# Shifted key and value copies moved from GpSimd to VectorE in a fused attention and mixer kernel

## The chip, the cores and the metric

The kernel runs on one core of a Trainium2 chip. The metric is the device time of one execution in microseconds (us). A core has five engines, each working through its own list of instructions strictly in order: TensorE (PE in the profile; its weight loads are listed apart as PEld), VectorE (DVE), ScalarE (ACT), GpSimd (POOL) and SyncE (SP). Engines wait for each other by semaphores. DMAs are issued from an engine's list too: here all loads from GpSimd's, the output stores from SyncE's.

## What is computed

First a windowed attention: 4 batches, 8 heads, 768 positions, head size 64. A query sees the first 8 positions (global) and the last 96 (local). Then a low-rank mixing over the positions and a two-layer channel network, both with a residual.

```python
scores = scale * np.matmul(q, k.transpose(0, 1, 3, 2))
is_global = pos[None, :] < int(n_global)              # 8
is_local = (rel >= 0) & (rel < int(n_local))          # 96
scores = np.where(keep, scores + bias, -1000000000.0)
a = softmax(scores)
x = a @ v                                             # heads side by side: (4, 768, 512)
h = xt @ U @ V                                        # xt: x with positions last; rank 32
u = x + h.transpose(0, 2, 1)
out = u + np.maximum(u @ w_ch1, 0.0) @ w_ch2          # 512 -> 2048 -> 512
```

(`softmax` stands here for the four lines that the reference writes out.)

## The kernel before

**Tiling.** The work of attention is cut into 16 pairs of heads, `pairs[i]`, four for each batch. The 768 positions are 6 blocks of 128. Since a query sees at most 96 positions back, a query block needs its own key block (the diagonal) and the last 96 positions of the block before it (the off-diagonal). The off-diagonal key block also has room for the global positions: `kP` (line 183) is a copy of the key tile `kT` in which, for each of 5 blocks, columns 32 to 127 are the block's own (line 184) and columns 0 to 31 are those of block 0 (line 185). `vp16` (lines 232 and 233) is the same for the values, in two buffers that alternate between pairs. Its source `v16` holds the values of 8 pairs, with a column of ones (line 141) that gives the softmax's sum.

**Steps of one pair**, by their functions: `load_pair` issues 6 DMAs from GpSimd (queries and keys, line 94, into `qkst`; values, line 100), each of which turns float32 into float16. `transposes` makes `qT` and `kT` on TensorE, which VectorE copies out of PSUM (lines 178 and 182), and then `kP`. `scores` multiplies (line 206) in three groups of blocks, the first of which reads `kP` alone; ScalarE takes the exponentials into `ep` (line 212), six activations for a pair. `mask` multiplies `ep` by the table of biases `expb` on VectorE (lines 224 and 227) and then makes `vp16`. `av` (lines 243 to 252) multiplies by the values, `norm` divides by the sum on VectorE (lines 266 and 270) and rounds to float16 on ScalarE (`x16`, line 275). `mix_tmp`, `mix_h` and `mix_t` are the low-rank step (lines 282 to 317).

**The channel network** is a queue of small pieces, `mlp_q`: for each batch 16 pieces of the first layer (`hps`, lines 329 and 335) and 24 of the second (`cps`, line 348, with the output at 354). `fill()` takes one piece off the queue and puts it between two steps of attention. The queue gets batch 0 at the end of iteration i = 4 of the main loop; before that, `fill()` does nothing. An iteration has ten calls of it, so a batch's 40 pieces go into four iterations. What is left at the end runs alone.

**The loop** (lines 372 to 400): iteration i does `mix_tmp` and `mix_h` of pair i - 1, `transposes` of pair i + 1, `av` and `norm` of pair i, `scores` and `mask` of pair i + 1, and `mix_t` of pair i - 1. Iteration -1 has only `transposes(0)`, `scores(0)` and `mask(0)`.

**Order.** For TensorE the order is that in which the code is written (line 369). On the other engines a scheduler lays the instructions out, from its own estimate of when each can start; within an engine nothing overtakes at run time. On GpSimd the program starts with the loads of pairs 0 to 3, the mixing matrices, the first layer's weights `w1_16` (line 152), pair 4 and the second layer's weights `w2_16` (line 155). The loads of a later pair wait until `transposes` has emptied a slot of `qkst`, which has 8.

**Tables.** `rel3` (lines 122 to 137) is built by GpSimd and VectorE, and `expb` from it on ScalarE (line 140); `mask` needs it.

In the profile names are shortened: `rel_106` is `rel3`, `v_81` is `v16`, `vp_82` is `vp16`, `w_16_79` and `w_16_80` are `w1_16` and `w2_16`, `x_...` with a number is `x16`, `tmp_...` with a number is `tmp16`, and `u_151` is `u16`.

Of the kernel before, what the change touches and what calls it, by code (L numbers as in the profile page):

```python
# [17 lines left out]
def kernel(  # L18
# [13 lines left out]
    nc = tc.nc  # L32
# [3 lines left out]
    P = 128  # L36
    G = 32
    DM = H * D
    NSB = S // P
    NPB = NSB - 1  # L40
# [7 lines left out]
    D1 = D + 1  # L48
# [20 lines left out]
    def ps_tp(name, dtype, cols):  # L69
        return psum.tile([P, cols], dtype, name=name, tag="tp", bufs=1)  # L70
# [95 lines left out]
    def transposes(i, which):  # L166
        stg = stage[i][which]
        tp = ps_tp("tp", FP16, NSB * P)
        for sb in range(NSB):
            nc.tensor.matmul(  # L170
                tp[:, sb * P:(sb + 1) * P],
                stg[:, sb].rearrange("s h d -> s (h d)"),
                ident16, is_transpose=True,
                start=(sb == 0), stop=(sb == NSB - 1),
            )
        if which == 0:
            qT = qkp.tile([P, S], FP16, name="qT", tag="qT")
            nc.vector.tensor_copy(qT, tp)
            qkT[i] = [qT]
        else:  # L180
            kT = qkp.tile([P, NSB, P], FP16, name="kT", tag="kT")
            nc.vector.tensor_copy(kT.rearrange("p n c -> p (n c)"), tp)  # L182
            kP = qkp.tile([P, NPB, P], FP16, name="kP", tag="kP")
            nc.gpsimd.tensor_copy(kP[:, :, G:P], kT[:, 0:NPB, G:P])  # L184
            nc.gpsimd.tensor_copy(  # L185
                kP[:, :, 0:G], kT[:, 0:1, 0:G].broadcast_to((P, NPB, G))
            )
            qkT[i] += [kT, kP]
# [28 lines left out]
    def mask(i):  # L217
        b, hp = pairs[i]
        ep = probs[i]
        for hi in range(2):  # L220
            h = 2 * hp + hi
            for j0, m in ((0, 2), (NPB, 1)):
                blk = ep[:, hi, j0:j0 + NPB]
                nc.vector.tensor_tensor(  # L224
                    blk, blk, expb[:, h, m:m + 1].broadcast_to((P, NPB, P)), ALU.mult
                )
        nc.vector.tensor_tensor(
            ep[:, :, NBK - 1], ep[:, :, NBK - 1], expb[:, 2 * hp:2 * hp + 2, 0], ALU.mult
        )
        vh = v16[:, i % VR]  # L230
        vp = vp16[:, i % 2]
        nc.gpsimd.tensor_copy(vp, vh[:, :, 0:NPB])
        nc.gpsimd.tensor_copy(vp[0:G], vh[0:G, :, 0:1].broadcast_to((G, 2, NPB, D1)))

    def av(i, hi):
        b, hp = pairs[i]
# [135 lines left out]
    for i in range(-1, NP + 1):  # L372
        if i + 6 < NP and i >= 0:
            load_pair(i + 6)
        if i >= 1:
            mix_tmp(i - 1)
            fill()
            mix_h(i - 1)
            fill()
        if i + 1 < NP:  # L380
            transposes(i + 1, 0)
            fill()
            transposes(i + 1, 1)
            fill()
        if 0 <= i < NP:
            av(i, 0)
            fill()
            av(i, 1)
            norm(i)
            fill()  # L390
        if i + 1 < NP:
            for ci in range(3):
                scores(i + 1, ci)
                fill()
            mask(i + 1)
        if i >= 1:
            mix_t(i - 1)
            fill()
            if i % NPAIR == 0:
                queue_batch(i // NPAIR - 1)  # L400
# [37 lines left out]
```

## Time and profile before

| what | us |
|---|---|
| median of two runs | 368.91 (368.76 to 369.07) |
| the profiled execution | 370.26 |
| its span, first to last instruction | 368.4 |
| TensorE busy | 269.3 (73%) |
| VectorE busy | 115.5 (31%) |
| ScalarE busy | 132.1 (36%) |
| GpSimd busy | 125.5 (34%) |

The granted TensorE clock is 1.00 throughout. The share of busy time hides that the run has stages. Here is the part of the page that cuts the span into 40 slices of 9.2 us; a digit is the busy share in tenths.

```profile
PE   1000055555559898999988999999899988777996
POOL 8994795674372507075060412011100000000000
```

TensorE does almost nothing in slices 2 to 5, is half busy in the next seven, and nine tenths busy from the thirteenth on; the digits 777 near the end are the last batch's first layer, which runs alone. GpSimd is busiest where TensorE is idle.

Rows of the other views read as follows. A timeline row: start, duration, engine, line, operation, output and input, shapes, count, and in brackets the idle time of the engine just before with what ended it. A row of the waits: who waited for whom, us in total, how many times, the longest.

### The profile page before, as it was taken

How to read it: one execution, taken by the hardware profiler on the slowest of the kernel's cores; microseconds unless marked ns; L12 is line 12 of the kernel's file. 1: busy time of each engine (PE TensorE's matmuls, PEld its weight loads, DVE VectorE, ACT ScalarE, POOL GpSimd, SP SyncE). 2: the span in 40 equal slices, each digit the busy share in tenths (PEclk: the TensorE clock that was granted, in tenths of full speed). 3: DMA queues.
4: the chain of work that ended last, by engine and by line, in shares of the span. 5: the costliest groups of instructions: out<-in, count | busy, mean ns of one | idle time of the engine just before them, and what ended most of it. 6: DMA issues, size and time to landing. Idle time of an engine off the chain costs nothing.

```text
span 368.4 us, 5118 instructions
## 1 busy us (share of the span) xinstructions
PE 269.3 (73%) x2080; PEld 147.0 (40%) x2080; DVE 115.5 (31%) x255; ACT 132.1 (36%) x265; POOL 125.5 (34%) x185
## 2 busy tenths in 40 slices
PE   1000055555559898999988999999899988777996
PEld 1000033444435455445444545545454544333442
DVE  1100054446442142555523254652322631000021
ACT  0400035432543654531547453235746200343100
POOL 8994795674372507075060412011100000000000
PEclk9999999999999999999999999999999999999999
DMA  9999999976591808297260601110000012000012
GB/s 69 105 122 204 187 171 60 64 52 41 38 67 11 55 0 55 39 120 71 62 44 0 41 5 59 59 47 11 0 2 0 34 53 85 2 0 0 30 57 85
DMA packets 82326, 20.34 MB, mean 55 GB/s; under 512 B 76640, under 2 KB 78720, under 8 KB 82304
## 3 DMA queue, kind: packets, MB, share of 16 engines
q0 software_dynamic: 78848, 13.74, 47.4%
q1 hardware_dynamic: 3456, 6.29, 4.6%
q8 instruction: 16, 0.26, 0.3%
q14 instruction: 6, 0.05, 0.1%
HBM read 27.46 MB, written 6.29 MB: 92 GB/s over the span
## 4 chain that ended last, share of the span: by engine, by line
PE 50%; ACT 17%; POOL 15%; DVE 8%; issue 5%; DMA 3%; POOLq 0%; ACTq 0%; DVEq 0%
PE cps L348 20%; PE hps L329 19%; ACT htr L335 13%; POOL qkst L94 7%; DMA w_16_79<-in_moe_w_ch_dram 3%; PE sc L206 3%; DVE ep L224 3%; POOL v_81 L100 3%; PE h_ps L294 2%; ACT ep L212 2%; PE tmp_ps L282 2%; DVE x_sb L299 2%; PE tp L170 1%; ACT uu L303 1%; POOL w_16_80 L155 1%
## 5 line engine op out<-in xcount | busy, mean ns | idle before, releaser
L329 PE MATMUL hps<-uT,w_16_79 128*128 128x384 f16 x512 | 105.4, 329 | 17.1 <-ACT htr L335 10.4
L348 PE MATMUL cps<-w_16_80,htr 128*128 128x512 f16 x384 | 93.1, 380 | 0.7 <-ACT htr L335 0.4
L335 ACT ACTIVATE htr<-hps 128x384 f16<-128x384 f32 x128 | 56.3, 487 | 82.6 <-PE hps L329 82.6
L329 PEld LDWEIGHTS <-w_16_79 128*128 128x128 f16 x512 | 49.4, 98 | 63.1 <-issue 38.7
L212 ACT ACTIVATE ep<-sc 128x512 f16<-128x512 f32 (+1 forms) x96 | 48.1, 563 | 50.0 <-PE sc L206 49.4
L224 DVE TENSOR_TENSOR ep<-ep,expb 128x640 f16<-128x640 f16 x64 | 30.6, 506 | 86.1 <-ACT ep L212 86.1
L94 POOL DMA_DIRECT2D qkst<-in_q_dram x32 | 26.9, 856 | 81.6 <-PE tp L170 80.8
L206 PE MATMUL sc<-qT,kP 64*128 64x128 f16 x160 | 12.7, 250 | 52.4 <-POOL kP L185 47.4
L348 PEld LDWEIGHTS <-htr 128*128 128x128 f16 x384 | 33.7, 98 | 35.3 <-issue 0.6
L354 DVE TENSOR_TENSOR osb<-cps,x_sb 128x512 f32<-128x512 f32 x24 | 16.6, 690 | 60.2 <-PE cps L348 59.7
L303 ACT ACTIVATE uu<-x_sb 128x768 f16<-128x768 f32 x16 | 13.5, 843 | 46.4 <-DVE x_sb L299 46.4
L206 PEld LDWEIGHTS <-kP 64*128 64x128 f16 x160 | 5.9, 108 | 56.1 <-POOL kP L185 49.4
L170 PE MATMUL tp<-ident_91,qkst 128*128 128x128 f16 x192 | 19.6, 251 | 11.7 <-POOL ident_91 L113 7.2
L100 POOL DMA_DIRECT2D v_81<-in_v_dram x32 | 26.8, 849 | 3.2 <-DMA w_16_79<-in_moe_w_ch_dram 3.0
L94 POOL DMA_DIRECT2D qkst<-in_k_dram x32 | 26.8, 861 | 2.8 <-PE tp L170 2.7
L184 POOL COPY kP<-kT 128x480 f16<-128x480 f16 x16 | 9.7, 608 | 50.8 <-DVE kT L182 50.8
L170 PEld LDWEIGHTS <-qkst 128*128 128x128 f16 x192 | 15.6, 113 | 17.4 <-issue 14.1
L299 DVE TENSOR_TENSOR x_sb<-x_sb,h_ps 128x768 f32<-128x768 f32 x16 | 15.3, 955 | 21.9 <-PE h_ps L294 21.9
L206 PE MATMUL sc<-qT,kT 64*128 64x128 f16 x192 | 15.0, 247 | 2.7 <-ACT ep L212 2.6
L270 DVE TENSOR_TENSOR x_sb<-ob,rcp 128x384 f32<-128x384 f32 x32 | 16.4, 552 | 0.0
L248 PE MATMUL ob<-vp_82,ep 128*128 128x65 f16 x160 | 16.1, 209 | 0.0
L252 PE MATMUL ob<-v_81,ep 128*128 128x65 f16 x160 | 16.1, 209 | 0.0
(103 smaller groups left out, 195.6 us busy)
## 6 DMA issues: line engine op xcount, KB each, us to landing
out_dram<-osb SPq DMA_DIRECT2D x24, 256.0 KB, 2.0
qkst<-in_q_dram POOLq DMA_DIRECT2D x32, 96.0 KB, 3.4
qkst<-in_k_dram POOLq DMA_DIRECT2D x32, 96.0 KB, 3.5
v_81<-in_v_dram POOLq DMA_DIRECT2D x32, 96.0 KB, 3.6
w_16_79<-in_moe_w_ch_dram POOLq DMA_DIRECT2D x4, 512.0 KB, 9.6
w_16_80<-in_moe_w_ch_dram POOLq DMA_DIRECT2D x8, 256.0 KB, 7.6
u_151<-in_moe_U_dram POOLq DMA_DIRECT2D x1, 48.0 KB, 3.5
v16w<-in_moe_V_dram POOLq DMA_DIRECT2D x1, 48.0 KB, 3.0
```

The costliest lines, as they stand in the source:

```text
L94: nc.gpsimd.dma_start(stg[:, :, hi], src[b, 2 * hp + hi].rearrange("(n p) d -> p n d", p=P),)
L100: nc.gpsimd.dma_start(v16[:, i % VR, hi, :, 0:D], v[b, 2 * hp + hi].rearrange("(n p) d -> p n d", p=P),)
L170: nc.tensor.matmul(tp[:, sb * P:(sb + 1) * P], stg[:, sb].rearrange("s h d -> s (h d)"), ident16, is_transpose=True, start=(sb == 0), stop ...
L206: nc.tensor.matmul(scs[hi][:, j * P:(j + 1) * P], lhsT, qT[r, t * P:(t + 1) * P], start=(j == 0), stop=(j == len(idx) - 1),)
L212: nc.scalar.activation(ep[:, hi, idx[0]:idx[0] + n].rearrange("p n c -> p (n c)"), scs[hi][:, 0:n * P], AF.Exp, scale=qk_scale,)
L224: nc.vector.tensor_tensor(blk, blk, expb[:, h, m:m + 1].broadcast_to((P, NPB, P)), ALU.mult)
L299: nc.vector.tensor_tensor(xp, xp, hps[:, 0:S].rearrange("p (n c) -> p n c", n=NSB), ALU.add)
L303: nc.scalar.activation(uu, xp, AF.Copy)
L329: nc.tensor.matmul(hh[f][:, 0:HT], w1_16[:, dc, jt * P:(jt + 1) * P], uTs[b][:, dc, f * HT:(f + 1) * HT], start=(dc == 0), stop=(dc == NDC ...
L335: nc.scalar.activation(htr[:, jt, f * HT:(f + 1) * HT], hh[f][:, 0:HT], AF.Relu)
L348: nc.tensor.matmul(cps, htr[:, jc, tt * P:(tt + 1) * P], w2_16[:, jc], start=(jc == 0), stop=(jc == NJC - 1),)
L354: nc.vector.tensor_tensor(osb, cps, xs[b][:, tt], ALU.add)
```

## The change

The four copies that make `kP` and `vp16` are issued to VectorE where they were issued to GpSimd. Nothing else in the code changes.

```diff
             kP = qkp.tile([P, NPB, P], FP16, name="kP", tag="kP")
-            nc.gpsimd.tensor_copy(kP[:, :, G:P], kT[:, 0:NPB, G:P])
-            nc.gpsimd.tensor_copy(
+            nc.vector.tensor_copy(kP[:, :, G:P], kT[:, 0:NPB, G:P])
+            nc.vector.tensor_copy(
                 kP[:, :, 0:G], kT[:, 0:1, 0:G].broadcast_to((P, NPB, G))
             )
...
         vh = v16[:, i % VR]
         vp = vp16[:, i % 2]
-        nc.gpsimd.tensor_copy(vp, vh[:, :, 0:NPB])
-        nc.gpsimd.tensor_copy(vp[0:G], vh[0:G, :, 0:1].broadcast_to((G, 2, NPB, D1)))
+        nc.vector.tensor_copy(vp, vh[:, :, 0:NPB])
+        nc.vector.tensor_copy(vp[0:G], vh[0:G, :, 0:1].broadcast_to((G, 2, NPB, D1)))
```

TensorE's list is the same before and after. Three other lists show what the scheduler made of it. Rows give line, operation, output, input and shape; the number behind a name tells instances apart (`kP_203` is pair 0's).

GpSimd before, where the copies of pair 0 stood: behind all loads of weights.

```order
L155 DMA w2_16_80<-in_moe_w_ch2_dram 128x2x512 x8
L100 DMA v16_81<-in_v_dram 128x6x64 x2
L184 COPY kP_203<-kT_201 128x5x96
L185 COPY kP_203<-kT_201 128x5x32
L232 COPY vp16_82<-v16_81 128x650
L100 DMA v16_81<-in_v_dram 128x6x64
L233 COPY vp16_82<-v16_81 32x650
```

GpSimd after, at the same place:

```order
L155 DMA w2_16_80<-in_moe_w_ch2_dram 128x2x512 x8
L94 DMA qkst_175<-in_q_dram 128x6x64 x2
L94 DMA qkst_178<-in_k_dram 128x6x64 x2
L100 DMA v16_81<-in_v_dram 128x6x64 x2
L94 DMA qkst_248<-in_q_dram 128x6x64 x2
L94 DMA qkst_251<-in_k_dram 128x6x64 x2
```

Only DMAs are left there, and the loads of pair 5 (`qkst_175`) follow at once.

VectorE before, at the program's start, from pair 0's key copy to its mask:

```order
L182 COPY kT_201<-tp_194 128x768
L134 COPY rel3_106<-rel3_106 128x128
L136 MEMSET rel3_106 32x128
L135 TENSOR_SCALAR rel3_106<-rel3_106 8x128
L137 MEMSET rel3_106 8x128
L141 MEMSET v16_81 128x96
L224 TENSOR_TENSOR ep_206<-ep_206,expb_125 128x640 x2
```

VectorE after, the same stretch:

```order
L182 COPY kT_201<-tp_194 128x768
L184 COPY kP_203<-kT_201 128x5x96
L185 COPY kP_203<-kT_201 128x5x32
L134 COPY rel3_106<-rel3_106 128x128
L136 MEMSET rel3_106 32x128
L135 TENSOR_SCALAR rel3_106<-rel3_106 8x128
L137 MEMSET rel3_106 8x128
L141 MEMSET v16_81 128x96
L232 COPY vp16_82<-v16_81 128x650 x2
L233 COPY vp16_82<-v16_81 32x650 x2
L224 TENSOR_TENSOR ep_206<-ep_206,expb_125 128x640 x4
```

The key copies of pair 0 stand right behind `kT`; the value copies of pairs 0 and 1 stand between the memset and the first mask.

ScalarE before, from pair 0's last exponential (its first rows, ahead of these, were the table load, the eight activations of line 140 and then line 212):

```order
L212 ACTIVATE ep_206<-sc_232 128x384
L275 ACTIVATE x16_306<-x_sb_300 128x768
L212 ACTIVATE ep_308<-sc_309 128x512
L212 ACTIVATE ep_308<-sc_310 128x512
L212 ACTIVATE ep_308<-sc_321 128x512
```

ScalarE after, the start and on to the same place:

```order
L212 ACT_TABLE_LOAD
L212 ACTIVATE ep_206<-sc_207 128x512
L140 ACTIVATE expb_125<-rel3_106 128x384 x8
L212 ACTIVATE ep_206<-sc_208 128x512
L212 ACTIVATE ep_206<-sc_219 128x512
L212 ACTIVATE ep_206<-sc_220 128x512
L212 ACTIVATE ep_206<-sc_231 128x384
L212 ACTIVATE ep_206<-sc_232 128x384
L212 ACTIVATE ep_308<-sc_309 128x512
L212 ACTIVATE ep_308<-sc_310 128x512
L275 ACTIVATE x16_306<-x_sb_300 128x768
L212 ACTIVATE ep_308<-sc_321 128x512
```

One exponential of pair 0 and the table load stand ahead of line 140, and in iterations 0 to 4 `x16` stands behind the second of the next pair's six exponentials, where it stood ahead of the first.

## The prediction

> **What bounds the kernel now.** I read the page first. Its chain of work that ended last gives the engines' shares of the span:
>
> ```profile
> PE 50%; ACT 17%; POOL 15%; DVE 8%; issue 5%; DMA 3%; POOLq 0%; ACTq 0%; DVEq 0%
> ```
>
> GpSimd does no arithmetic of weight, yet 15% of the chain is its own. Next I read the waits, and then TensorE's timeline:
>
> ```profile
> PE sc L206 <- POOL kP L185: 47.4, 6, 37.2
> ```
>
> ```profile
> 46.61 0.71 PE L206 MATMUL sc<-qT,kP 64*128 64x128 f16 x9 [37.17 <-POOL kP L185]
> ```
>
> TensorE's scores wait 47.4 us for GpSimd's `kP`, 37.2 of them once, before pair 0. GpSimd's and VectorE's timelines tell why:
>
> ```profile
> 24.03 2.33 POOL L152 DMA_DIRECT2D w_16_79<-in_moe_w_ch_dram  x4
> ...
> 45.70 0.60 POOL L184 COPY kP<-kT 128x480 f16<-128x480 f16 x1
> ```
>
> ```profile
> 9.48 0.56 DVE L182 COPY kT<-tp 128x768 f16<-128x768 f16 x1 [0.89 <-PE tp L170]
> 12.84 0.29 DVE L134 COPY rel_106<-rel_106 128x128 f32<-128x128 f32 x1 [2.81 <-POOL rel_106 L130]
> 13.22 0.64 DVE L135 TENSOR_SCALAR rel_106<-rel_106 8x128 f32<-8x128 f32 x1
> 13.70 0.17 DVE L137 MEMSET rel_106<- 8x128 f32 x1
> 15.16 0.14 DVE L141 MEMSET v_81<- 128x96 f16 x1 [1.30 <-issue]
> ```
>
> `kT` of pair 0 is there at 9.48 + 0.56 = 10.04. Its copy starts at 45.70, since the weights' loads are ahead of it on GpSimd. So the first 46 us are GpSimd's issuing, not arithmetic.
>
> From there to the first `hps` there is no channel work to fill gaps, and an iteration is one chain through all engines. Here is pair 4's, on VectorE, GpSimd, TensorE and ScalarE in turn:
>
> ```profile
> 82.61 1.87 DVE L224 TENSOR_TENSOR ep<-ep,expb 128x640 f16<-128x640 f16 x4 [2.96 <-ACT ep L212]
> ...
> 89.58 0.56 DVE L182 COPY kT<-tp 128x768 f16<-128x768 f16 x1 [0.96 <-PE tp L170]
> 90.73 0.27 DVE L266 RECIPROCAL rcp<-ob 128x6 f32<-128x6 f32 x2 [0.58 <-PE ob L252]
> 90.96 1.02 DVE L270 TENSOR_TENSOR x_sb<-ob,rcp 128x384 f32<-128x384 f32 x2
> 94.92 1.87 DVE L224 TENSOR_TENSOR ep<-ep,expb 128x640 f16<-128x640 f16 x4 [2.94 <-ACT ep L212]
> ```
>
> ```profile
> 89.84 1.66 POOL L94 DMA_DIRECT2D qkst<-in_k_dram  x2
> 91.47 0.62 POOL L184 COPY kP<-kT 128x480 f16<-128x480 f16 x1
> ```
>
> ```profile
> 92.40 0.71 PE L206 MATMUL sc<-qT,kP 64*128 64x128 f16 x9 [1.71 <-POOL kP L185]
> ```
>
> ```profile
> 92.07 0.84 ACT L275 ACTIVATE x_683<-x_sb 128x768 f16<-128x768 f32 x1 [2.98 <-DVE x_sb L270]
> 93.10 3.14 ACT L212 ACTIVATE ep<-sc 128x512 f16<-128x512 f32 x6 [0.19 <-PE sc L206]
> ```
>
> `kT` ends at 90.14, `kP` starts at 91.47 behind two loads, scores start at 92.40, exponentials at 93.10, and the mask at 94.92, when the third exponential is done (0.61 each). The stage ends here, on the chain's own view:
>
> ```profile
> 107.64 1.87 DVE ep L224 x4
> ...
> 111.03 2.67 PE hps L329 x8
> ```
>
> Behind it TensorE has its filler. The window of 111 to 310 us (PE, PEld, DVE, ACT and POOL busy):
>
> ```profile
> 111.00:310.00 199.00, 185.42 (x1466) 97.30 (x1466) 76.62 (x168) 87.65 (x179) 45.73 (x68) 1.00 0.30 38
> ```
>
> There TensorE is busy 185.4 of 199 us; the chain has left GpSimd. So the change is worth what it does before 111.03.
>
> **The change, part by part.** I write M(i) for the start of pair i's first mask product (line 224). M(3) to M(5) are the 82.61, 94.92 and 107.64 above, and after M(5) come 111.03 - 107.64 = 3.39 us to the first `hps`.
>
> *The pair of key copies on VectorE.* No row shows a float16 copy within SBUF on VectorE. The nearest is line 134's float32 copy of 128 columns, 0.29 us: two of these are 0.58, and the first copy has 480 columns. The low end is two memsets like line 141's, 0.28; the high end is two like line 135's 0.64 (an odd duration for 128 columns; see the rivals), 1.28. I take 0.8, near the copy row with something for the longer first one. VectorE: DVE Perf Modes in the Trainium skill, in its section on the TRN2 errata, puts a VectorE copy at 58 cycles plus columns over four; by that I estimate 0.19 and 0.10 us, and the sum below would come out 2.6 us lower. No row here can tell which.
>
> *The start.* `kP` of pair 0 stands right behind `kT`: 10.04 + 0.8 = 10.84. Scores follow at once, the first exponential 0.70 later (92.40 to 93.10), done near 12.2. Then ScalarE waits for `rel3`, ready at 13.70 + 0.17 = 13.87 as before, since GpSimd's list is unchanged up to there. Line 140 took this long, and before it the table load, which now lies in idle time:
>
> ```profile
> 13.97 1.28 ACT L140 ACT_TABLE_LOAD   x1 [13.97 <-DVE rel_106 L137]
> 15.26 3.41 ACT L140 ACTIVATE expb<-rel_106 128x384 f16<-128x384 f32 x8
> ```
>
> So `expb` is done at 13.9 + 3.41 = 17.3, two more exponentials at 18.5, and M(0) = 18.5. The value copies of pairs 0 and 1 stand between 15.3 and there on VectorE: on GpSimd such a pair took
>
> ```profile
> L232 POOL COPY vp_82<-v_81 x16: 730/734/766, 46.5 to 257.7; 128x650 f16<-128x650 f16 x16
> L233 POOL COPY vp_82<-v_81 x16: 721/739/1057, 48.0 to 258.5; 32x650 f16<-32x650 f16 x16
> ```
>
> that is 1.47, so two pairs are at most 2.9 and end by 18.2; hidden, with 0.3 to spare. Before, M(0) was 49.08:
>
> ```profile
> 49.08 1.49 DVE L224 TENSOR_TENSOR ep<-ep,expb 128x640 f16<-128x640 f16 x2 [33.77 <-ACT ep L212]
> ...
> 59.44 1.87 DVE L224 TENSOR_TENSOR ep<-ep,expb 128x640 f16<-128x640 f16 x4 [4.07 <-ACT ep L212]
> 61.22 0.28 DVE L227 TENSOR_TENSOR ep<-ep,expb 128x256 f16<-128x256 f16 x1
> 61.42 0.27 DVE L286 CAST tmp_365<-tmp_ps 32x128 f16<-32x128 f32 x1
> ...
> 63.45 0.55 DVE L178 COPY qT<-tp 128x768 f16<-128x768 f16 x1
> 64.89 0.56 DVE L182 COPY kT<-tp 128x768 f16<-128x768 f16 x1 [0.89 <-PE tp L170]
> ```
>
> *From `kT` to the next mask*, the new tail of every iteration: key copies 0.8, handover 0.05, scores to exponential 0.70, three exponentials 1.82 (93.10 to 94.92), and now `x16` among them, 0.84, since on ScalarE's list it stands behind the second. Sum 4.21. Before, the tail was 90.14 to 94.92, 4.78. So ScalarE's new order gives back most of what GpSimd's loads cost: the wait of 1.33 us goes, and `x16`, which lay in that wait, is late next.
>
> *Iterations.* M(0) to M(1): 1.98 for the mask (59.44 to 61.42), 2.00 from `qT` to the end of `kT` (63.45 to 65.45), 4.21: 8.19, so M(1) = 26.7. M(1) to M(2): 59.44 to 65.45 is 6.01, plus 4.21: M(2) = 36.9. The next three: 82.61 to 90.14 is 7.53, plus 4.21 = 11.74 each (12.31 before), so M(5) = 72.1, and `hps` starts at 75.5 in place of 111.03: 35.5 earlier.
>
> *The value copies inside an iteration* stand behind `norm` and ahead of the mask. `norm` ends 0.8 + 0.27 + 1.02 = about 2.05 after `kT`, the mask can start at 4.21: 2.16 of cover for at most 1.47. I cost them at nothing; without that cover each iteration would pay up to 1.47.
>
> *Loads.* GpSimd's list loses only copies, so no load is issued later. The last issues of `w2`, and the slowest median time to landing on the page (9.6 us):
>
> ```profile
> 42.37 1.51 POOL L155 DMA_DIRECT2D w_16_80<-in_moe_w_ch_dram  x2 [0.37 <-issue]
> ```
>
> ```profile
> w_16_79<-in_moe_w_ch_dram POOLq DMA_DIRECT2D x4, 512.0 KB, 9.6
> ```
>
> The latest load that matters is pair 5's: its first issue comes behind the last of `w2`, at 42.37 + 1.51 = 43.9, its sixth 0.83 x 5 later, near 48; with those 9.6 us it is there by 58. `transposes(5)` follow M(4) = 60.4 by some 5 us.
>
> *From `hps` on*, 368.4 - 111.03 = 257.4 us. VectorE gets about 11 more sets of copies there. The first value copy stands ahead of `norm`'s reciprocal, and ScalarE's `x16` waits for `norm` with the network's activations behind it. Pair 5:
>
> ```profile
> 123.42 1.02 DVE L270 TENSOR_TENSOR x_sb<-ob,rcp 128x384 f32<-128x384 f32 x2
> ```
>
> ```profile
> 125.17 0.83 ACT L275 ACTIVATE x_1001<-x_sb 128x768 f16<-128x768 f32 x1
> ```
>
> `x_sb` was done at 124.44 and used at 125.17: 0.73 of slack against a copy of 0.5 (a mask product's 1.87 / 4) to 0.85 (one load's issue, half of 1.66). That is 0 to 0.12 us, eleven times: I take 0.5 in all.
>
> *Sum.* 75.5 + 257.4 + 0.5 = 333.4 us of span against 368.4. The profiled execution was 370.26, but the median of the runs is 368.91, 0.5 above the span; so 333.9, rounded to 334.
>
> **The rivals.**
>
> *VectorE's copies stall beside GpSimd's loads.* Two issues of loads, and a cast beside the first:
>
> ```profile
> 7.04 1.70 POOL L94 DMA_DIRECT2D qkst<-in_q_dram  x2
> ...
> 12.93 1.71 POOL L94 DMA_DIRECT2D qkst<-in_q_dram  x2
> ```
>
> ```profile
> 7.15 0.21 DVE L124 CAST rel_106<-reli 128x128 f32<-128x128 int32 x1
> ```
>
> For it speaks line 135, eight partitions by 128 columns, 0.64 us, ending 13.86, just as a load's issue that began at 12.93 (half of 1.71) ended; against it line 124, 0.21 us wholly inside the other.
>
> And the loads sit at the wrong place: they are released by the same transposes that precede `kP` (89.84 above). If every copy waits out one issue of 0.85, the key copies cost 0.58 + 1.7 = 2.28, 1.48 more in each of five iterations, 7.4; the value copies 1.24 + 1.7 = 2.94 against 2.16 of cover, 3.9 in all. 334 + 11 = 345. SBUF — State Buffer in the Trainium skill says so in its section on who interferes with whom: GpSimd and VectorE share a pair of ports that the one takes from the other for a whole instruction. By that rule it would be 345; of the two rows above one agrees and one does not.
>
> *The network's part gains too*, since its iterations also had `kP` behind loads. TensorE idles 13.6 us between 111 and 310; if half went, 327. Against it: the waits for `kP` other than the first come to 10.2 us in 5 times, which the stage before 111 uses up.
>
> *Data come late.* If pair 5's loads or the weights trail by some 6 us more than in the sum above, what is gained stops there: each us later adds one; 340.
>
> *Slower or the same.* VectorE's first value copy ahead of `norm` delays `x16`, and with it the network's activations. It decides from the point where it eats the 35 us: 35 / 11 = 3.2 us beyond the slack of 0.73, in each of eleven iterations, a copy of nearly 4 us, where GpSimd took 0.74. That would end at 369 or above.
>
> **How the numbers follow.** Forecast, 334, with its own range of 330 to 339 (key copies at their ends give 331.4 and 336.4; the rest is the network's part, either way): 0.70. Stalls, up to 345: 0.17. More gain: 0.05. Late data: 0.05. Slower or the same: 0.03. The range 330 to 346 holds the forecast, most of the stalls and the late data. All but the last case are far beyond 2%, which is about what a measurement of this kernel can tell from no change: faster 0.96, same 0.02, slower 0.02.
>
> **What would show it.** Right: TensorE's first `sc` near 11 us in place of 46.61, M(0) near 18.5, steps of about 8, 10 and 12 us, the first `hps` near 75, then 257 us as before; GpSimd gone from the chain but for the first loads. Wrong in size: key copies over 1.3 us in the timeline while a load is issued, or a wait for a DMA ahead of `tp`. Wrong in mechanism: the first `hps` early and the part behind it longer by as much.

## The result, and the profile after

The changed kernel takes 331.69 us (median of two runs, 331.17 to 332.2) against 368.91: a ratio of 0.8991, with a 95% interval of 0.8929 to 0.9053. Four later runs of the same kernel, listed with the experiments below, have a median of 331.75 and a ratio of 0.8965 to 0.8997. The span of the profiled execution is 329.4 us against 368.4, so 39.0 us went.

The page of the changed kernel, first the slices of TensorE and GpSimd, then the chain by engine:

```profile
PE   0256557669898999998999999989999897777995
POOL 8997478996105051221030000000000000000000
...
PE 54%; ACT 19%; DVE 10%; POOL 7%; DMA 5%; issue 4%; ACTq 0%; POOLq 0%; DVEq 0%
```

TensorE now works from the second slice on (a slice is 8.2 us here), though GpSimd is as busy there as it was: TensorE's scores no longer wait for its copies. GpSimd's share of the chain is 7% where it was 15%. TensorE's timeline has the first scores at 10.67 us, 35.9 us earlier:

```profile
10.67 0.71 PE L206 MATMUL sc<-qT,kP 64*128 64x128 f16 x9 [1.24 <-DVE kP L185]
```

The first mask product of pairs 0 to 5, on VectorE's timeline:

```profile
18.37 1.87 DVE L224 TENSOR_TENSOR ep<-ep,expb 128x640 f16<-128x640 f16 x4 [1.72 <-ACT ep L212]
...
26.09 1.87 DVE L224 TENSOR_TENSOR ep<-ep,expb 128x640 f16<-128x640 f16 x4 [1.22 <-ACT ep L212]
...
35.70 1.87 DVE L224 TENSOR_TENSOR ep<-ep,expb 128x640 f16<-128x640 f16 x4 [1.09 <-ACT ep L212]
...
46.95 1.87 DVE L224 TENSOR_TENSOR ep<-ep,expb 128x640 f16<-128x640 f16 x4 [0.98 <-ACT ep L212]
...
58.20 1.87 DVE L224 TENSOR_TENSOR ep<-ep,expb 128x640 f16<-128x640 f16 x4 [0.94 <-ACT ep L212]
...
69.25 1.87 DVE L224 TENSOR_TENSOR ep<-ep,expb 128x640 f16<-128x640 f16 x4 [0.77 <-ACT ep L212]
```

These are M(0) to M(5), with steps of 7.72, 9.61, 11.25, 11.25 and 11.05 us. Each wait in brackets is now for ScalarE's exponential. The first `hps` follows 3.39 us behind M(5), exactly as before. Here it is on the chain, start, duration and what:

```profile
72.64 2.66 PE hps L329 x8
```

So 111.03 - 72.64 = 38.4 of the 39.0 us came ahead of the first `hps`. Behind it are 329.4 - 72.64 = 256.8 us, against 257.4. The window that answers to the one of 111 to 310 us before (PE, PEld, DVE, ACT and POOL busy):

```profile
74.00:273.00 199.00, 184.40 (x1469) 96.84 (x1467) 86.36 (x205) 87.65 (x180) 27.11 (x34) 1.00 0.34 42
```

TensorE is busy 184.4 of 199 us there, 185.4 before: that stage neither gained nor lost. GpSimd's 27.1 us were 45.7.

Where an iteration's time goes now, on the chain from `kT` of pair 3 to its mask:

```profile
42.60 0.57 DVE kT L182
...
43.19 0.56 DVE kP L184
43.75 0.12 DVE kP L185
...
43.91 0.65 PE sc L206 x8
...
44.61 1.08 ACT ep L212 x2
45.70 0.73 ACT x_555 L275
46.43 0.50 ACT ep L212
...
46.95 1.47 DVE ep L224 x3
```

From the end of `kT` (43.17) to the mask (46.95) are 3.78 us. `x16` stands between the second exponential and the third, as the prediction had it, and costs 0.73.

The copies themselves, a tile's groups with the least, the median and the longest in ns, then the groups by cost with busy us and mean ns:

```profile
L184 DVE COPY kP<-kT x16: 307/310/609, 10.1 to 237.1; 128x480 f16<-128x480 f16 x16
L185 DVE COPY kP<-kT x16: 184/192/437, 10.4 to 237.3; 128x160 f16<-128x160 f16 x16
```

```profile
L232 DVE COPY vp_82<-v_81 128x650 f16<-128x650 f16 x16 | 5.7, 363 | 18.9 <-PE ob L252 18.8
L233 DVE COPY vp_82<-v_81 32x650 f16<-32x650 f16 x16 | 5.7, 361 | 0.2
```

A key copy takes 0.31 and 0.19 us when nothing disturbs it, and up to twice that in some instances; the experiments ask why.

### The profile page after: what moved, and what is told of

Read it like the earlier page. It is cut to its first block, busy times and chain, and to the rows that moved or that the text cites. A ratio compares the mean times of both kernels' runs of the same rounds, so it can differ in the third digit from the quotient of the medians.

```text
span 329.4 us, 5112 instructions
## 1 busy us (share of the span) xinstructions
PE 268.0 (81%) x2080; PEld 146.6 (45%) x2080; DVE 132.4 (40%) x319; ACT 130.7 (40%) x265; POOL 90.1 (27%) x121
## 4 chain that ended last, share of the span: by engine, by line
PE 54%; ACT 19%; DVE 10%; POOL 7%; DMA 5%; issue 4%; ACTq 0%; POOLq 0%; DVEq 0%
PE cps L348 23%; PE hps L329 21%; ACT htr L335 15%; POOL qkst L94 4%; DMA w_16_79<-in_moe_w_ch_dram 3%; DVE x_sb L299 3%; PE sc L206 3%; DVE ep L224 2%; PE h_ps L294 2%; POOL v_81 L100 2%; PE tmp_ps L282 2%; ACT ep L212 2%; DMA w_16_80<-in_moe_w_ch_dram 2%; ACT uu L303 2%; PE tp L170 1%
## 5 line engine op out<-in xcount | busy, mean ns | idle before, releaser
L224 DVE TENSOR_TENSOR ep<-ep,expb 128x640 f16<-128x640 f16 x64 | 29.6, 490 | 38.7 <-ACT ep L212 38.7
L94 POOL DMA_DIRECT2D qkst<-in_q_dram x32 | 27.1, 865 | 65.3 <-PE tp L170 63.4
L354 DVE TENSOR_TENSOR osb<-cps,x_sb 128x512 f32<-128x512 f32 x24 | 16.5, 688 | 59.7 <-PE cps L348 59.2
L206 PEld LDWEIGHTS <-kT 64*128 64x128 f16 x192 | 7.9, 104 | 23.8 <-issue 23.2
L182 DVE COPY kT<-tp 128x768 f16<-128x768 f16 x16 | 8.9, 558 | 18.9 <-PE tp L170 18.9
```

The lines of the kernel that those rows point to most:

```text
L94: nc.gpsimd.dma_start(stg[:, :, hi], src[b, 2 * hp + hi].rearrange("(n p) d -> p n d", p=P),)
L206: nc.tensor.matmul(scs[hi][:, j * P:(j + 1) * P], lhsT, qT[r, t * P:(t + 1) * P], start=(j == 0), stop=(j == len(idx) - 1),)
L224: nc.vector.tensor_tensor(blk, blk, expb[:, h, m:m + 1].broadcast_to((P, NPB, P)), ALU.mult)
L354: nc.vector.tensor_tensor(osb, cps, xs[b][:, tt], ALU.add)
```

## The experiments

The ratios stand against runs of the kernel before on the same chip, with 95% intervals. "Span" is that of the profiled execution. Line numbers in the profiles of the two kernels with repeated copies are one higher than elsewhere, since a loop's line stands ahead.

**The change again**, as a reference for the others.

> The changed kernel once more, for a narrower interval and as the base of the three beside it: 331 to 332.

331.75 us (331.33 to 331.99), ratio 0.8981 (0.8965 to 0.8997), span 329.6.

**Keys alone.** From the changed kernel, the value copies back on GpSimd.

```diff
-        nc.vector.tensor_copy(vp, vh[:, :, 0:NPB])
-        nc.vector.tensor_copy(vp[0:G], vh[0:G, :, 0:1].broadcast_to((G, 2, NPB, D1)))
+        nc.gpsimd.tensor_copy(vp, vh[:, :, 0:NPB])
+        nc.gpsimd.tensor_copy(vp[0:G], vh[0:G, :, 0:1].broadcast_to((G, 2, NPB, D1)))
```

> Only the key copies on VectorE, the value copies stay on GpSimd. Theory (place in GpSimd's list): the first value copy now stands behind the weights and pair 5's loads, near 51 us, so the product with the values of pair 0 is near 53, M(1) near 57, then steps of 9.6 and three of 11.3 as in the changed kernel: first hps near 104, time 360 to 362. Rival (the key copies are what holds the kernel, the value copies are a detail): M(0) near 18 and first hps near 73 as in the changed kernel, time 330 to 334.

365.36 us (365.08 to 366.03), ratio 0.9881 (0.9854 to 0.9907), span 363.3. M(0) came at 18.05, as early as with the whole change, but M(1) only at 56.50. TensorE's timeline says why:

```profile
52.28 0.21 PE L248 MATMUL ob<-vp,ep 128*128 128x65 f16 x1 [30.78 <-POOL vp L233]
```

The wait of 37 us for `kP` had become one of 30.8 for `vp16`, whose copies stood behind the weights' loads in the same way. So the mechanism is the expected one, but the time is 3 to 5 us above the expectation. The steps from M(1) on show where, on VectorE's timeline and GpSimd's beside it:

```profile
62.52 0.56 DVE L182 COPY kT<-tp 128x768 f16<-128x768 f16 x1 [0.89 <-PE tp L170]
63.12 0.70 DVE L184 COPY kP<-kT 128x480 f16<-128x480 f16 x1
63.74 0.79 DVE L185 COPY kP<-kT 128x160 f16<-128x160 f16 x1
```

```profile
62.85 1.66 POOL L94 DMA_DIRECT2D qkst<-in_k_dram  x2
```

The two key copies end 1.41 us after they began, where they need 0.42 undisturbed, while GpSimd issues two loads. The steps from M(1) on are 11.12, 12.01 and 12.00 us, where the whole change has 9.61, 11.25 and 11.25, and the first `hps` comes at 106.23, 2.2 us after the expected 104; the rest of the excess is about the 1.8 us by which a time exceeds its span in these runs. That is the rival of stalls, in another kernel than the one it was named for.

**Values alone.** From the changed kernel, the key copies back on GpSimd.

```diff
-            nc.vector.tensor_copy(kP[:, :, G:P], kT[:, 0:NPB, G:P])
-            nc.vector.tensor_copy(
+            nc.gpsimd.tensor_copy(kP[:, :, G:P], kT[:, 0:NPB, G:P])
+            nc.gpsimd.tensor_copy(
```

> Only the value copies on VectorE, the key copies stay on GpSimd. Theory: kP of pair 0 still starts near 45.7, M(0) near 49, each later kP behind four loads; GpSimd is rid of 1.5 us per pair, M(1) some 2 us earlier: time 364 to 369. Rival (each part carries about half of the gain): near 350.

371.14 us (370.41 to 372.08), ratio 1.0036 (1.0021 to 1.0051), span 369.4: slower than before by a third of a per cent, where a small gain was expected. `kP` of pair 0 stands behind the weights again, M(0) is 48.27, and the last three steps are 12.86, 12.83 and 13.36 us against 12.31, 12.31 and 12.72. TensorE still waits for GpSimd's `kP`, and behind it ScalarE has `x16`, one exponential further back than in the kernel before:

```profile
92.22 0.71 PE L206 MATMUL sc<-qT,kP 64*128 64x128 f16 x9 [1.72 <-POOL kP L185]
```

```profile
92.92 0.60 ACT L212 ACTIVATE ep<-sc 128x512 f16<-128x512 f32 x1 [4.01 <-PE sc L206]
93.42 0.83 ACT L275 ACTIVATE x<-x_sb 128x768 f16<-128x768 f32 x1
94.15 2.43 ACT L212 ACTIVATE ep<-sc 128x512 f16<-128x512 f32 x5
```

An iteration pays the wait for `kP`, in which `x16` used to lie, and `x16` too. So one half of the change is worth 4.3 us (369.69 - 365.36), the other costs 1.4, and both together are worth 38: each set of copies was a gate by itself behind the same loads, and one open gate is not a way through.

**Loads behind the copies, everything on GpSimd.** From the kernel before: the loads of pairs 2 and 3 and the mixing matrices at the end of iteration -1, those of pair i + 4 at the end of iteration i, the weights at the ends of iterations 2 to 4. All four copies stay on GpSimd.

```diff
-    load_pair(2)
-    load_pair(3)
...
-    for c in range(NDC):
-        nc.gpsimd.dma_start(w1_16[:, c], w1v[:, c])
-    load_pair(4)
-    for c in range(0, NJC, 2):
-        nc.gpsimd.dma_start(w2_16[:, c:c + 2], w2v[:, c:c + 2])
-    load_pair(5)
+    def load_later(i):
+        if i == -1:
+            load_pair(2)
+            load_pair(3)
...
+        elif i + 4 < NP:
+            load_pair(i + 4)
+        if i == 2:
+            for c in range(NDC):
+                nc.gpsimd.dma_start(w1_16[:, c], w1v[:, c])
+        if i == 3 or i == 4:
+            for c in range(8 * (i - 3), 8 * (i - 2), 2):
+                nc.gpsimd.dma_start(w2_16[:, c:c + 2], w2v[:, c:c + 2])
...
-        if i + 6 < NP and i >= 0:
-            load_pair(i + 6)
...
+        load_later(i)
```

> All copies stay on GpSimd, but the loads of pairs 2 and on and of the weights are issued from the loop, behind the copies of the first pairs. Theory (it is the place in the list, not the engine's speed): kP of pair 0 at 13.0, M(0) near 21; kP(1) and kP(2) still behind some 12 loads each, near 29 and 42; first hps at 83 to 86, time 341 to 345. Rival (GpSimd's slower copies, 0.95 against 0.49 us a pair of key copies, are what is gained): within 2% of before, 362 or more.

345.54 us (345.25 to 345.84), ratio 0.9342 (0.9318 to 0.9366), span 343.5, the first `hps` at 86.57; time and `hps` are each about half a microsecond above the expected range. GpSimd's timeline, the key copies of pairs 0 and 1 (line 184 is 190 there):

```profile
12.94 0.64 POOL L190 COPY kP<-kT 128x480 f16<-128x480 f16 x1
...
28.38 0.69 POOL L190 COPY kP<-kT 128x480 f16<-128x480 f16 x1
```

With no arithmetic moved to another engine, 369.69 - 345.54 = 24.1 of the 38 us are there. The place of the copies in GpSimd's list is the larger part of the effect; what is left, 13.8 us, came only with the change of engine: GpSimd's list still delays them here (28.38 for pair 1, 22.39 with the change), and its copies are longer (0.64 us beside 0.31). How much of the 13.8 each of the two has, no run shows.

**Key copies three times.** To price VectorE's key copies, from the changed kernel:

```diff
-            nc.vector.tensor_copy(kP[:, :, G:P], kT[:, 0:NPB, G:P])
...
+            for _ in range(3):
+                nc.vector.tensor_copy(kP[:, :, G:P], kT[:, 0:NPB, G:P])
...
```

> The changed kernel with each pair of key copies issued three times. Theory (key copies are on the path before the first hps and hidden behind it): 2 x 0.49 us more in each of five iterations, first hps at 77.5 in place of 72.6, the part behind it 257 as before: 336 to 337. Rival (VectorE holds the network's part too): another 1 us in each of the ten later iterations, near 346.

337.03 us (336.73 to 337.2), ratio 0.9111 (0.9088 to 0.9134), span 334.8, the first `hps` at 77.40 and 257.4 us behind it. The span is 5.4 us longer; of these, 4.8 lie ahead of the first `hps` and 0.6 in the 257 us behind it, though ten pairs' copies were tripled there. So a key copy costs its time while there is no channel work for TensorE, and next to nothing afterwards.

**`x16` on VectorE.** The chain names `x16` as what is late next, so, from the changed kernel:

```diff
-        nc.scalar.activation(x16, x_sb[:, :, hp * P:(hp + 1) * P], AF.Copy)
+        nc.vector.tensor_copy(x16, x_sb[:, :, hp * P:(hp + 1) * P])
```

> The changed kernel with the rounding of line 275 (x16) on VectorE. Theory (x16 on ScalarE's list stands ahead of the third exponential and is on the path): 0.73 less in each of five iterations, first hps near 69 in place of 72.6; behind it 0.75 less in each of the six iterations in which x16 stands between two activations of the first layer, 252 in place of 257: 323 to 325. Rival (x16 lies in a wait, as before): within 1 us of the changed kernel.

325.92 us (325.67 to 325.97), ratio 0.8820 (0.8806 to 0.8833), span 324.1. The total is above the expected end by 0.9, and its parts are not as expected: the first `hps` at 72.0, where the theory had 69. M(1) to M(3) were early (25.58, 34.66, 45.20), M(4) was not:

```profile
56.52 0.50 DVE L232 COPY vp<-v 128x650 f16<-128x650 f16 x1 [1.96 <-DMA v<-in_v_dram]
56.94 0.54 DVE L275 CAST x<-x_sb 128x768 f16<-128x768 f32 x1
57.40 0.61 DVE L233 COPY vp<-v 32x650 f16<-32x650 f16 x1
57.94 1.67 DVE L224 TENSOR_TENSOR ep<-ep,expb 128x640 f16<-128x640 f16 x4
```

VectorE's list has a value copy ahead of M(4) whose values had not landed: late data, the third rival, appears as soon as the rest is 2 us faster. The part behind `hps` gave the 4.7 us of the theory (324.1 - 72.0 = 252.1, against 256.8).

**Both roundings on VectorE.** The same, and line 303:

```diff
-        nc.scalar.activation(uu, xp, AF.Copy)
+        nc.vector.tensor_copy(uu, xp)
```

> As the last, and line 303 (uu) on VectorE too. Theory: uu is on the path before the first layer's activations in some six iterations behind the first hps (0.84 each, the page's chain shows it), and is off it before the first hps, where it now stands ahead of kT on VectorE's list at up to 0.9 but in the time of the transposes: 319 to 324. Rival (VectorE's list is then too full ahead of kT): slower than with x16 alone by 1 to 4 us.

324.26 us (323.83 to 324.38), ratio 0.8774 (0.8760 to 0.8788), span 322.6: just above the range of the theory, and not slower as the rival had it. The first `hps` is at 71.3, with the same wait for values (1.57 us) ahead of M(4) at 57.70. Windows of the changed kernel and of this one, from about the first `hps` to the end (busy as above):

```profile
73.00:329.40 256.40, 230.58 (x1688) 118.23 (x1686) 90.51 (x211) 101.47 (x211) 28.11 (x35) 1.00 0.29 39
```

```profile
72.00:322.60 250.60, 229.59 (x1687) 118.06 (x1685) 102.39 (x234) 84.96 (x188) 29.82 (x37) 1.00 0.31 41
```

TensorE's work is the same 230 us; ScalarE has 16.5 us less, VectorE 11.9 more, and from the first `hps` to the end it is 251.3 us in place of 256.8. Nearly all of this had come with `x16` alone (252.1). Moving `uu` as well gave 0.8 us behind the first `hps` and 0.7 ahead of it, where the theory had it on the path in some six iterations at 0.84 us each. Both roundings take 0.84 us on ScalarE, so what such an instruction costs depends on its place in the list and not only on its length. Why `uu` gave so little no run here shows.

**Pair 5's loads ahead of the second layer's weights**, on top of both roundings:

```diff
     load_pair(4)
+    load_pair(5)
     for c in range(0, NJC, 2):
         nc.gpsimd.dma_start(w2_16[:, c:c + 2], w2v[:, c:c + 2])
-    load_pair(5)
```

> Version with both roundings on VectorE, and pair 5's six loads ahead of the eight loads of the second layer's weights on GpSimd's list. Theory (late data): in the version with both roundings VectorE's value copy of pair 5 stands ahead of M(4) and starts at 56.30 after a wait of 1.57 for its DMA, whose issue ended at 50.73. Six issues earlier by eight weights' issues the values land some 6 us sooner, the wait goes, M(4) comes near 56.1 (57.70 before), the first hps near 69.7 (71.3), the span near 321 and the median at 322 to 323. Weights that land some 5 us later, near 58, are still read only after 80. Rival (the wait only moves, to another load or to VectorE's list itself): M(4) stays at 57 to 58 and the median at 324 to 324.6.

323.20 us (322.33 to 323.32), ratio 0.8747 (0.8722 to 0.8772), span 320.6, the first `hps` at 69.91. This is the lowest time of all versions. The same place on VectorE's timeline:

```profile
54.50 0.32 DVE L232 COPY vp<-v 128x650 f16<-128x650 f16 x1
54.74 0.85 DVE L275 CAST x<-x_sb 128x768 f16<-128x768 f32 x1
55.51 0.31 DVE L233 COPY vp<-v 32x650 f16<-32x650 f16 x1
55.75 1.86 DVE L224 TENSOR_TENSOR ep<-ep,expb 128x640 f16<-128x640 f16 x4
```

The wait is gone. M(4) is 1.95 us earlier; 0.33 of that is there at M(3) already, and the step from M(3) to M(4), 10.53 where it was 12.15, has the rest, about as much as the wait. The first `hps` is 1.4 earlier (the step to M(5) is 10.76 where it was 10.33). The spans of the profiled executions differ by the 2 us that were expected, but the new one is the fastest of its four; the median fell by 1.1 and ended just above the range of the theory. The two versions ran on different chips and the intervals of their ratios overlap, so the evidence that it was pair 5's values is the step and the wait, and that the edit moved nothing but the order of loads.

**Keys alone, with more slots.** To take the stalls out of the first experiment, its staging tiles got 12 slots, so that loads need not wait for the transposes that precede the key copies.

```diff
-            stg = stp.tile([P, NSB, 2, D], FP16, name="qkst", tag="qkst", bufs=8)
+            stg = stp.tile([P, NSB, 2, D], FP16, name="qkst", tag="qkst", bufs=12)
```

> The kernel with only the key copies on VectorE, and 12 slots in place of 8 for the staged queries and keys, so that the loads aren't released by the transposes that precede a key copy. Theory (a VectorE copy waits out a load's issue on GpSimd): key copies of pairs 2 to 4 at 0.5 in place of 1.41 us, steps near 11.1 in place of 12.0, time 362 to 363 in place of 365.4. Rival (the copies are slow for another reason, such as the columns or the TensorE beside them): copies still 1.4, time 365 to 366.

365.52 us (364.89 to 366.03), ratio 0.9892 (0.9873 to 0.9911), span 363.1: no change. GpSimd ran ahead until 12 slots were full too, and for pairs 3 to 5 the loads came once more with the copies (0.71 and 0.78 us, steps of 12.0). Only pair 2's copies were nearly free of them, 0.42 and 0.19 us, with a step of 10.38 in place of 11.12, as the theory has it; pair 5's, which had been free, were held instead. The edit did not do what it was made for, so its time decides nothing.

**Sixteen copies.** This one asks the question of the stalls directly: line 184's copy sixteen times in pair 1, beside a row of loads without a gap, and in pair 14, beside none.

```diff
-            nc.vector.tensor_copy(kP[:, :, G:P], kT[:, 0:NPB, G:P])
+            for _ in range(16 if i in (1, 14) else 1):
+                nc.vector.tensor_copy(kP[:, :, G:P], kT[:, 0:NPB, G:P])
```

> The changed kernel, with line 184's copy issued sixteen times in pair 1 (near 22 us, where GpSimd issues loads without a pause) and in pair 14 (where GpSimd does nothing). Theory (a copy within SBUF that begins later than some 0.2 us into the issue of a load waits for the issue's end): in pair 14 every copy takes 0.31 and they follow each other by 0.34, 5.4 us in all; in pair 1 short copies of 0.31 and long ones of 0.5 to 0.8 alternate, the long ones end within 0.15 us of the end of an issue, and the sixteen take 6.3 to 8 us as long as the issues last. Rival (the long copies have another cause, so GpSimd's issues do not matter): both sets look alike, 5.4 us each, or the long ones end anywhere in an issue. Time: 6 to 7.5 us more from pair 1, 0 to 5 from pair 14, 338 to 344 in all; the rival would give 337 to 342.

338.01 us in a single run, span 336.2, the first `hps` at 78.98: 6.3 us from pair 1, half a microsecond from pair 14. VectorE's timeline, some long ones of pair 1 by themselves, and a run of eleven in pair 14:

```profile
22.99 0.78 DVE L185 COPY kP<-kT 128x480 f16<-128x480 f16 x1
...
26.96 0.45 DVE L185 COPY kP<-kT 128x480 f16<-128x480 f16 x1
...
27.79 0.48 DVE L185 COPY kP<-kT 128x480 f16<-128x480 f16 x1
...
222.21 3.74 DVE L185 COPY kP<-kT 128x480 f16<-128x480 f16 x11
```

GpSimd's timeline, the issues beside the first three:

```profile
22.73 0.91 POOL L148 DMA_DIRECT2D u<-in_moe_U_dram  x1
...
26.30 1.01 POOL L94 DMA_DIRECT2D qkst<-in_q_dram  x1
27.30 0.85 POOL L94 DMA_DIRECT2D qkst<-in_q_dram  x1
```

The eleven in pair 14 follow each other by 0.34 us. In pair 1 the long ones end at 23.77, 27.41 and 28.27, and the issues at 23.64, 27.31 and 28.15: 0.13, 0.10 and 0.12 us before. In the run of nine copies from 26.64 on, one short copy gets through between two long ones, so beside the loads of 0.83 us two copies pass in each issue. The sixteen took 6.7 us in pair 1, against 16 x 0.34 = 5.4 without loads. The size is at the low end of the theory, and the long ones of that run took only 0.45 to 0.48, since they began 0.5 to 0.7 us into an issue; the ends are where the theory put them, and the rival, that both sets look alike, has fallen.

## Why the prediction was right, point by point

**What bounds the kernel.** Right, and shown: 38.4 of 39.0 us came ahead of the first `hps`, and the copies' place in GpSimd's list alone gives 24.1 of them with nothing moved to VectorE. What the prediction did not say is that the two sets of copies are gates in a row; the two halves of the change, worth 4.3 and -1.4 us alone, show it.

**The start.** M(0) 18.5, measured 18.37. Its terms hold: `kP` ready at 10.60 (10.84), scores at 10.67, the table load in idle time, line 140 as before. The value copies of pairs 0 and 1 took 1.4 us in place of at most 2.9, hidden.

**The key copies.** 0.8 us, measured 0.42 from start to end when undisturbed (0.31 and 0.19, overlapping); in pairs 1 to 5 it was 0.67, 0.42, 0.68, 0.67 and 0.42, in all 2.9 against 4.0. Line 134's row twice, 0.58, with nothing added, would have given the 2.9. By the Trainium skill's VectorE: DVE Perf Modes, in the section on the TRN2 errata, 58 cycles and columns over four, they were 0.19 and 0.10; the runs show 0.31 and 0.19, so the measurement decides against that figure, but the same section adds that a single copy was measured above it.

**The tail.** 4.21 us, measured 3.78 in pair 3. Besides the copies (0.68 for 0.8) the exponentials and `x16` were mis-sized: 1.82 + 0.84 = 2.66 in the sum, 1.08 + 0.73 + 0.50 = 2.31 on the chain. Where ScalarE's instructions follow each other directly they overlap: `x16`, listed with 0.84, moves the next one back by 0.73. Those two terms, 1.1 us for the copies and about 1.7 for ScalarE over five iterations, make up the 75.5 - 72.64 = 2.9 us by which the first `hps` came earlier than forecast. The order that the prediction read there, `x16` behind the second exponential, stands as it said, and deserved its term: with it on VectorE the step from M(0) to M(1) fell from 7.72 to 7.21. One reading was off: the prediction has 12.31 for each of the last three steps before, but the last, 94.92 to 107.64, was 12.72.

**The value copies** were costed at nothing behind 2.16 us of cover, and the waits of the mask are all for ScalarE, 0.77 us at the least. In this kernel that holds. With `x16` on VectorE too the cover is used up, and from M(2) on the mask waits for VectorE's own list.

**Loads.** That none is late was right for this kernel by luck. The prediction looked at `transposes(5)`, which need pair 5's queries and keys by 65, and had the data there by 58. The first to need pair 5's data is VectorE's value copy, which the scheduler put ahead of M(4). VectorE's rows of the changed kernel, and the last issue of pair 5's values:

```profile
55.29 1.02 DVE L270 TENSOR_TENSOR x_sb<-ob,rcp 128x384 f32<-128x384 f32 x2
56.34 0.56 DVE L232 COPY vp_82<-v_81 128x650 f16<-128x650 f16 x1
```

```profile
50.01 0.82 POOL L100 DMA_DIRECT2D v_81<-in_v_dram  x1 [0.67 <-DMA w_16_80<-in_moe_w_ch_dram]
```

From that issue to the landing the trace has 6.2 us, so the values were there near 56.2. The copy, behind `norm`, was due at about the same moment: nothing was to spare. Two microseconds less elsewhere made it wait 1.96. The experiment that moved pair 5's loads shows that this was the cause.

**From `hps` on.** 257.4 + 0.5 forecast, 256.8 measured; busy TensorE is the same within 1 us in 199, so neither the half microsecond for delayed `x16` nor the rival's gain of 6.8 came.

**From the span to the time.** The sum gave a span of 333.4 us, and the measured one is 329.4, so it was 4.0 too long: 2.9 ahead of the first `hps` and 1.1 behind it. The time missed by only 333.9 - 331.69 = 2.2, and that is partly luck. The prediction added 0.5 us to get from the span to the time, taking the span of one execution before and the median of two others. The same execution's time was 370.26 for its span of 368.4, and 331.17 for 329.4 after: some 1.8 in both.

**Stalls.** The rival had the mechanism right and its size wrong. Three of the ten key copies of pairs 1 to 5 were held up, by 0.25 us each; it assumed 0.85 for every copy. The two rows that seemed to contradict each other do not: line 135 (0.64 us) began 0.29 us into an issue, line 124 (0.21 us) 0.11 into one, and below some copies that begin that early pass. The case in which it does cost is the kernel with the keys alone, whose key copies took 1.41 us.

**Slower or the same.** `x16` was not delayed by the value copies: the copy ahead of `norm` takes 0.33 us, behind the first `hps` `x16` starts 0.53 after `norm` (85.79 to 86.32), and the price of 3.2 us per iteration was never near.

## What to carry to other kernels

An engine that both issues loads and makes small copies gives every copy the place in its list, whatever the copy costs: ask of each copy what stands ahead of it there, and open all gates behind the same loads at once, or nothing is seen. When a wait goes, read from the other engines' lists what now comes second (here a rounding on ScalarE, then values that land 2 us late), because these were worth some 8.5 us more together, 331.75 down to 323.2. And a sum of durations from a timeline is too long where instructions of one engine follow each other directly; the chain's steps are the better terms.

## What the runs showed of the hardware that was not expected

A VectorE copy within SBUF may stall beside a load's issue on GpSimd, and when it does it ends with the issue, not after a time of its own. A key copy of 480 columns ended 0.10 to 0.14 us behind the issue's end, whether it had begun early in it (0.78 us for the one at 22.99) or late (0.45 for the one at 26.96); the copy of 160 columns in the kernel with the keys alone ended 0.02 behind it (64.53 and 64.51). But not every copy beside an issue stalls. In the sixteen, short copies that came 0.14 to 0.16 us after an issue's end, when the next was already listed as running, took their own 0.31 us, and so two copies passed in each issue. One at 26.64 took 0.29 us, though the issue of 26.30 had been listed for a third of a microsecond, and beside the four issues of weights (24.05 to 26.35) the copies took no more than 0.37.

The section on who interferes with whom, in SBUF — State Buffer of the Trainium skill, has a pair of ports shared by the two engines and held for a whole instruction by the one that comes first. The stalled copies agree with that; the free ones inside an issue do not, unless GpSimd takes the ports only some time after its issue begins. Where that border lies is open: in the kernel with the keys alone the second key copy, which could begin at most 0.16 us into the second load (the first was done at 63.82, that load began at 63.66), stalled, while in the sixteen ones that began 0.15 and 0.19 us into an issue did not. VectorE's copies out of PSUM show no stall: all sixteen that make `kT` took 0.557 or 0.558 us in the changed kernel, with loads issued beside them (as at 21.80) or without.
